# Attention: scores directly behind the transposes of the probabilities, wider products, small products at the end of the iteration

## The chip, the cores and the metric

The kernel runs on one core of one Trainium2 chip. The metric is the time of the device for one execution, in microseconds, as the median of several runs. Three runs of the kernel before took 557.59, 556.81 and 554.96 us.

## The reference

Sliding-window attention with sink tokens is followed by a soft mixture of experts and a feed-forward layer, all in fp32:

```python
scores = (q @ k.T) / 8                      # B=4, H=8, S=768, D=64
keep = (pos_k < 4) | ((0 <= pos_q - pos_k) & (pos_q - pos_k < 128))
a = softmax(where(keep, scores, -1e9));  x = a @ v           # x: 3072 x 512
logits = x @ phi                            # 3072 x 32 slots (8 experts of 4)
d = softmax(logits, over tokens);   slot_in = d.T @ x
slot_out[e] = relu(slot_in[e] @ w1[e]) @ w2[e]               # w1: 512 x 1024
x = softmax(logits, over slots) @ slot_out
h = x @ w_in;   out = (h - tanh(h)) @ w_out                  # d_ff = 2048
```

With a window of 128, a tile of 128 queries needs the keys of its own tile and of the tile before, and the 4 sink keys.

## The kernel before, in words

**Stages.** The attention stage works on pairs of heads, 16 in all (4 batches of 4 pairs). While it runs, expert weights are loaded into slots of a ring. Behind it come the experts' first product (`ffn1`, L1000), which frees slots for the remaining weights (`refill`, L968), the second (L1106), and the feed-forward layer (L1258 and around it).

**Iterations.** The attention loop (L760) has 48 iterations, three to a pair; each handles two query tiles of 128 for both heads. It is written as a pipeline in which the engines get their instructions in the order of the code, and each engine runs its own in that order. Iteration `i` issues, in this order:

- `trans(i-4)` (L661): four 128x128 transposes of normalized probabilities on TensorE into the one buffer `pT`; VectorE multiplies them by the two triangle masks (L667) and copies the middle blocks (L670). `pb_of` says where this goes.
- `exps(i-2)` (L621): on ScalarE, four exponentials with sums (L628) and two small operations.
- `turn_tasks` (L547): transposes of x (`x_trans`, L337) from a queue `xq`, each with a copy by ScalarE (L343), and those steps of a batch's tail that are transposes.
- a step of the conversion of `w_in` on VectorE and ScalarE (`conv_step`).
- `do_logits` (L724): the logits of a finished pair (L351), added up by VectorE (L356).
- `run_tasks` (L556): the other steps of a batch's tail: products with sink values, maximum, exponentials, slot inputs (L432, L437).
- `scores(i)` (L560): the products of queries and keys into two of the three buffers `sc`.
- `copies(i)` (L600): the scores go to SBUF with the window's masks (L611 on ScalarE, L612 and L608 on VectorE), and VectorE takes the maximum (L618).
- `norm(i-2)` (L633): a reciprocal on VectorE and the multiplication by it on GpSimd (L640).
- `avs(i-5)` (L672): the products of probabilities and v, which add up in two banks over the three iterations of a pair; behind the third, ScalarE copies them out (L709) and the pair is queued for logits one iteration later and for transposes of x two later.

The small products share two buffers of PSUM, `mi` (`misc`, L314): a third one waits until the first has been copied out.

**Shapes.** Scores are products of 64x64 quadrants (two heads by two row halves, four run side by side). For the first half of a tile's queries one matmul takes all of its two or three key blocks of 66 columns (64 keys and 2 sinks), with an output in steps; for the second half there is one matmul of 66 columns to a block. In `avs`, a block of v (`own`) is the weight for the probabilities of its own tile and of the next one, partly as one matmul of 128 columns and partly as two of 64; the blocks of v with their halves swapped (`other`, from `swapped`) take the middle blocks. In fp32 each matmul is two MATMUL and two LDWEIGHTS instructions.

Of the kernel before, what the change touches and what calls it, by code (L numbers as in the profile page):

```python
# [28 lines left out]
P = 128  # L29
SINK, WIN = 4, 128  # L30
CH = P + SINK
KW = 6 * CH + 2
HB = CH // 2
# [94 lines left out]
def tile_kernel(ctx: ExitStack, tc: tile.TileContext, qk, vv, v0, v0t, nw, phi, w1, w2,  # L128
# [17 lines left out]
    def run(ctx, fast):  # L146
# [35 lines left out]
        def sv(slot, lo, n, dt=F32):  # L182
            if slot in HALF:
                return slots[slot][lo // 1024][:, lo % 1024:lo % 1024 + n].bitcast(dt)
            return slots[slot][0][:, lo:lo + n].bitcast(dt)
# [59 lines left out]
        def attention(fast):  # L245
            nqk = {}
            swapped = [{}, {}]
            VS = (((11, 1552, 0, 3), (12, 1584, 3, 3)), ((10, 1536, 0, 4), (11, 768, 4, 2)))
            with ExitStack() as c2:
                ap = c2.enter_context(tc.tile_pool(name="ap", bufs=1))  # L250

# [279 lines left out]
                def kslc(a, lo, n):  # L531
                    return a[:, S + lo:S + lo + n]

                NQ = B * NP_ * 3

                def pb_of(i):
                    return sv(10, 768 * (i % 3), 768) if i % 3 < 2 else sv(11, 0, 768)

                Zs, sc_t, av, small, sus = {}, {}, {}, {}, {}

# [1 line left out]
                cur = [[]]  # L542
# [4 lines left out]
                def turn_tasks():  # L547
                    n = 0
                    while cur[0] and cur[0][0].__name__ in ("t_pst", "t_trd", "t_trl"):
                        cur[0].pop(0)()  # L550
                        n += 1
                    while n < 2 and xq and xq[0][0] <= now[0] and xq[0][1] <= done[0] and len(xq) > 2 * n:
                        xq.pop(0)[2]()
                        n += 1

                def run_tasks():  # L556
                    while cur[0]:
                        cur[0].pop(0)()

                def scores(i):  # L560
                    pb, m = divmod(i, 3)
                    a = nqk[pb][0]
                    n = (i + ZO) % 5
                    z = z4 if n == 4 else sv(11, 1024, 4 * CH) if n == 3 else sv(12, 4 * CH * n, 4 * CH)
                    Zs[i] = z
                    sc_t[i] = [pp.tile([P, 512], F32, name="sc", tag="sc", bufs=3) for u in range(2)]
                    for jj in range(2):
                        for n in range(3):
                            for u in range(2):
                                t = 2 * m + u  # L570
                                lo = CH * (t - 1) + (CH + 2 if t == 0 and jj else 68 if jj else 0)
                                if t == 0 and jj == 0:
                                    lo = 0
                                s_ = sc_t[i][u]
                                if jj == 0:
                                    if n:
                                        continue
                                    k, o = (3 if t else 2), 0
                                    dst = [[CH, k], [1, HB]]
                                    w_ = HB * k  # L580
                                else:
                                    if t == 0 and n == 2:
                                        continue
                                    o = (198, 66)[n] if t == 0 else (330, 198, 66)[n]
                                    dst = [[1, HB]]
                                    lo, w_ = lo + HB * n, HB
                                j = 2 * t + jj
                                for hh in range(2):
                                    r, w = (slice(64 * x, 64 * x + 64) for x in (hh, hh ^ u))
                                    d = s_[w, o:]  # L590
                                    PE.matmul(bass.AP(d.tensor, d.offset, [list(d.ap[0])] + dst), a[r, 64 * j:64 * j + 64],  # L591
                                              kslc(a, lo, w_)[r, :], start=True, stop=True)

                def halves(x, o, n):
                    return bass.AP(x.tensor, x.offset + o, [list(x.ap[0]), [2 * CH, 2], [1, n]])
# [65 lines left out]
                def trans(i, tag="pT"):  # L661
                    Z = Zs.pop(i)
                    pt = pp.tile([P, 512], F32, name=tag, tag=tag, bufs=1 if tag == "pT" else 3)
                    for n in range(4):
                        PE.transpose(pt[:, P * n:P * n + P], Z[:, CH * n + 2:CH * n + 130], ident)  # L665
                    d = pb_of(i)
                    DVE.tensor_tensor(d[:, 0:512].rearrange("p (l c) -> p l c", l=2),  # L667
                                      bass.AP(pt.tensor, pt.offset, [list(pt.ap[0]), [0, 2], [1, 256]]),
                                      c_t[:, C_ML:C_ML + 512].rearrange("p (l c) -> p l c", l=2), op=ALU.mult)
                    DVE.tensor_copy(d[:, 512:768], pt[:, 256:512])  # L670

                def avs(i):  # L672
                    pb, m = divmod(i, 3)
                    b, p = divmod(pb, NP_)
                    v, vs, d = nqk[pb][1], swapped[pb % 2], pb_of(i)
                    if m == 0:
                        av[pb] = [pp.tile([P, 512], F32, name=f"av{x}", tag=f"av{x}", bufs=1) for x in range(2)]
                    t0 = 2 * m

                    def mm(a, w, src, u, n=1):  # L680
                        for hh in range(2):
                            k, r = (slice(64 * x, 64 * x + 64) for x in (a, hh))
                            x = d[k, src + P * u + 64 * (hh ^ u):]
                            x = bass.AP(x.tensor, x.offset, [list(x.ap[0]), [256 + P + 64 - P * hh, n], [1, 64]])
                            o = 64 * (t0 + u)
                            PE.matmul(av[pb][a][r, o:o + 64 * n], w(k, r), x, start=m == 0 and n == 2, stop=m == 2 and src == 512,  # L686
                                      skip_group_check=True)

                    def own(t):
                        return lambda k, r: v[k, t, r]  # L690

                    def other(t):
                        return lambda k, r: vs[t][k, r]

                    for a in range(2):
                        mm(a, own(t0), 0, 0, 2)
                    for a in range(2):
                        mm(a, own(t0 + 1), 0, 1)
                    if m:
                        for a in range(2):  # L700
                            mm(a, own(t0 - 1), 256, 0)
                    for u in range(2):
                        for a in range(2):
                            if t0 + u - 1 + a >= 0:
                                mm(a, other(t0 + u - 1 + a), 512, u)
                    if m == 2:
                        x = xt_t[p]
                        for a in range(2):
                            ACT.copy(x.rearrange("p (t a c) -> p a t c", a=2, c=64)[:, a],  # L709
                                     av[pb][a][:, 0:384].rearrange("p (t c) -> p t c", c=64))  # L710
                        xT[b, p] = x
                        lq.append((i + LAG + 1 + LD, b, p))
                        xq.append((i + LAG + 1 + XD, b, lambda: x_trans(b, p, 0, 4)))
                        xq.append((i + LAG + 1 + XD, b, lambda: x_trans(b, p, 4, 2)))
                        if p == NP_ - 1:
                            if b < B - 1:
                                a, late2[:] = tail_tasks(b)
                                steps.extend(a)
                                if b < B - 2:
                                    steps.append([lambda: done.__setitem__(0, b + 1)])  # L720
# [3 lines left out]
                def do_logits():  # L724
                    if lq and lq[0][0] <= now[0]:
                        logits(*lq.pop(0)[1:])
# [33 lines left out]
                for i in range(NQ):  # L760
                    now[0] = i
                    next_step()
                    k = i - LAG
# [2 lines left out]
                    k -= 1  # L766
                    if i >= 2:
                        exps(i - 2)
                    turn_tasks()
                    while stage[0] < min(3 * NC + 1, (i - 2) * CVR):  # L770
                        conv_step(stage[0])
                        stage[0] += 1
                    do_logits()
                    run_tasks()
                    scores(i)
                    if i < NQ - 3:
                        filler(sc_t[i][1], NE_ if i < NK else NF)
# [20 lines left out]
                    if k >= 0:  # L798
                        avs(k)
                        if k % 3 == 2 and k // 3 + 2 < B * NP_:  # L800
                            load_v(k // 3 + 2)
                    if i % 3 == 1 and pre:
                        ring_dma(pre.pop(0))
                    if i % 3 == 0 and i // 3 < 16 - NC:
# [656 lines left out]
```

## Time and profile before

| | |
|---|---|
| median of three runs | 556.81 us |
| the profiled execution | 558.53 us |
| its span | 556.7 us |
| mean granted clock of TensorE, as a share of full speed | 0.981 |

One execution was profiled. Times count from the start of its span. PE is TensorE's matmuls and PEld its weight loads, which lie over each other; DVE is VectorE, ACT ScalarE, POOL GpSimd, and SP issues the transfers. `out<-in` are the program's names without buffer numbers (`w` is a slot of the ring, which attention uses for its buffers too; `mi`, `sc`, `av`, `pT` are PSUM). Square brackets give the idle time ahead of a group and what ended it; "issue" means that the engine waited for nothing that the profile shows.

### The profile page before, as it was taken

The page shows a single profiled execution, that of the slowest core. Times are in us where ns is not written, and L with a number is a line of the kernel's source. Part 1 is how long each engine was busy: PE and PEld are TensorE (multiplying, and loading weights), DVE is VectorE, ACT ScalarE, POOL GpSimd, SP SyncE. Part 2 cuts the span into 40 slices and gives each one's busy share as a digit, 9 for nine tenths or more (in the row PEclk, how much of TensorE's full clock was granted, in tenths as well). Part 3 has the DMA queues.
Part 4 walks back from the last instruction along what each step waited for, and adds up shares of the span by engine and source line. Part 5 has one row for each costly group of instructions (what it writes and reads, how often), then busy time and mean ns, then how long its engine had stood idle before and what let it go on. Part 6 is the DMA issues. An engine that isn't in the chain of part 4 may idle for free.

```text
span 556.7 us, 14342 instructions
## 1 busy us (share of the span) xinstructions
PE 502.6 (90%) x5634; PEld 378.2 (68%) x5634; DVE 367.2 (66%) x752; ACT 301.8 (54%) x924; POOL 270.6 (49%) x337
## 2 busy tenths in 40 slices
PE   8788778778788989888999999999999999999996
PEld 5566665666666643325677777788888888888884
DVE  3598785878868648769998887545454454445441
ACT  4689886878889535245654554434343343334331
POOL 0465845746564300005878887654443443443441
PEclk9799998989989999999999999999999999999999
DMA  8988987454447889994223000210020010001002
GB/s 304 414 308 312 334 326 262 157 161 167 149 161 288 294 328 377 408 410 145 83 75 114 2 1 1 88 64 1 0 77 1 1 70 7 1 1 76 1 1 79
DMA packets 26618, 84.16 MB, mean 151 GB/s; under 512 B 3378, under 2 KB 7602, under 8 KB 24626
## 3 DMA queue, kind: packets, MB, share of 16 engines
q1 hardware_dynamic: 26546, 83.20, 41.1%
q8 instruction: 45, 0.74, 0.5%
q14 instruction: 27, 0.22, 0.1%
HBM read 76.90 MB, written 6.29 MB: 149 GB/s over the span
## 4 chain that ended last, share of the span: by engine, by line
PE 65%; DMA 10%; DVE 9%; ACT 7%; POOL 4%; issue 4%; SPq 1%; POOLq 0%; ACTq 0%; DVEq 0%
PE o L1258 42%; DMA w<-in_w 7%; PE sc L591 5%; PE h L1168 4%; PE av L686 3%; PE pT L665 3%; ACT w L628 2%; POOL w L640 2%; DMA w<-in_vv 1%; ACT xt L709 1%; PE mi L432 1%; DVE mx L618 1%; DVE g L1237 1%; DMA w<-in_w_in 1%; DVE y L1235 1%
## 5 line engine op out<-in xcount | busy, mean ns | idle before, releaser
L1223 POOL TENSOR_TENSOR gl<-g,gh 128x512 fp32r<-128x512 f32 x96 | 124.0, 1292 | 119.8 <-ACT gh L1222 119.0
L1258 PE MATMUL o<-whi,gh 128*128 128x512 f32 x384 | 152.0, 396 | 4.1 <-POOL wlo L1069 1.2
L1258 PE MATMUL o<-wlo,gh 128*128 128x512 f32 x384 | 151.1, 394 | 1.7 <-POOL wlo L1069 1.7
L1218 ACT ACTIVATE u<-h 128x512 f32<-128x512 f32 x96 | 57.5, 599 | 147.5 <-PE h L1168 147.4
L1235 DVE SCALAR_TENSOR_TENSOR y<-u,h 128x512 f32<-128x512 f32 x96 | 66.7, 695 | 100.3 <-ACT u L1218 100.3
L1258 PE MATMUL o<-whi,gl 128*128 128x512 f32 x384 | 108.3, 390 | 0.1
L1258 PEld LDWEIGHTS o<-whi,gh 128*128 128x128 f32 x384 | 72.3, 188 | 23.5 <-POOL wlo L1069 1.5
L1258 PEld LDWEIGHTS o<-wlo,gh 128*128 128x128 f32 x384 | 72.2, 188 | 18.8 <-POOL wlo L1069 2.4
L1258 PEld LDWEIGHTS o<-whi,gl 128*128 128x128 f32 x384 | 72.1, 188 | 16.2 <-POOL gl L1223 0.8
L640 POOL TENSOR_TENSOR w<-w,su 128x528 f32<-128x528 f32 x38 | 41.2, 1084 | 67.3 <-DVE su L635 52.1
L1237 DVE SCALAR_TENSOR_TENSOR g<-u,y 128x512 f32<-128x512 f32 x96 | 65.8, 685 | 7.0
L1222 ACT CAST gh<-g 128x512 fp32r<-128x512 f32 x96 | 58.9, 613 | 5.7 <-DVE g L1237 5.5
L628 ACT ACTIVATE w<-w,nb 128x132 f32<-128x132 f32 x152 | 59.7, 394 | 1.2
L591 PE MATMUL sc<-w 64*64 64x66 f32 (+2 forms) x1472 | 49.5, 262 | 5.9 <-DVE w L608 2.8
L591 PEld LDWEIGHTS sc<-w 64*64 64x64 f32 x1472 | 39.7, 140 | 21.5 <-issue 12.4
L686 PE MATMUL av<-w,w 64*64 64x64 f32 (+1 forms) x1408 | 42.3, 243 | 7.0 <-issue 7.0
L686 PEld LDWEIGHTS av<-w,w 64*64 64x64 f32 x1408 | 36.4, 141 | 9.1 <-issue 8.4
L1068 POOL TENSOR_SCALAR whi<-wf 128x512 fp32r<-128x512 f32 x16 | 9.9, 620 | 63.0 <-DMA w<-in_w_out 59.3
L1168 PE MATMUL h<-cT,wst 96*128 96x512 f32 x96 | 37.8, 395 | 0.9 <-DVE wst L1156 0.9
L611 ACT COPY w<-sc 128x264 f32<-128x264 f32 x63 | 21.5, 378 | 27.5 <-PE sc L591 19.2
L665 PE MATMUL pT<-c_t,w 128*128 128x128 f32 x148 | 25.9, 298 | 9.1 <-POOL w L640 7.1
L667 DVE TENSOR_TENSOR w<-pT,c_t 128x512 f32<-128x512 f32 x46 | 30.6, 666 | 4.0 <-PE pT L665 3.9
(250 smaller groups left out, 731.3 us busy)
## 6 DMA issues: line engine op xcount, KB each, us to landing
w<-in_w SPq DMA_DIRECT2D x32, 512.0 KB, 10.2
w<-in_w SPq DMA_DIRECT2D x14, 1024.0 KB, 8.1
w<-in_qk SPq DMA_DIRECT2D x16, 781.0 KB, 6.0
w<-in_w_out SPq DMA_DIRECT2D x15, 512.0 KB, 3.6
w<-in_vv SPq DMA_DIRECT2D x16, 384.0 KB, 4.7
w<-in_w_in SPq DMA_DIRECT2D x8, 512.0 KB, 4.6
w<-in_vv SPq DMA_DIRECT2D x16, 192.0 KB, 5.8
out<-xt SPq DMA_DIRECT2D x12, 256.0 KB, 2.1
```

Of the source, the lines that this page charges most:

```text
L591: PE.matmul(bass.AP(d.tensor, d.offset, [list(d.ap[0])] + dst), a[r, 64 * j:64 * j + 64], kslc(a, lo, w_)[r, :], start=True, stop=True)
L628: ACT.activation(z, z, AF.Exp, bias=nb[:, u:u + 1], scale=SCALE, accum_out=su[:, u, :])
L640: (POOL if i < NQ - 1 else DVE).tensor_tensor(z, z, f, op=ALU.mult)
L665: PE.transpose(pt[:, P * n:P * n + P], Z[:, CH * n + 2:CH * n + 130], ident)
L686: PE.matmul(av[pb][a][r, o:o + 64 * n], w(k, r), x, start=m == 0 and n == 2, stop=m == 2 and src == 512, skip_group_check=True)
L1168: PE.matmul(h_of(s), w_of(f), cT[0:G3, CK * c:CK * c + CK], start=True, stop=True)
L1218: ACT.activation(u_b[s % 3], h_of(s), AF.Square)
L1222: ACT.copy(gh, g)
L1223: POOL.tensor_tensor(gl, g, gh.bitcast(F32), op=ALU.subtract)
L1235: DVE.scalar_tensor_tensor(y_t, u, c0 / c1, h, op0=ALU.add, op1=ALU.mult)
L1237: DVE.scalar_tensor_tensor(g, u, c1, y_t, op0=ALU.mult, op1=ALU.mult)
L1258: PE.matmul(acc[t], a[:, P * t:P * t + P], w, start=start, stop=stop)
```

## The change

In the loop, the order within an iteration is now: transposes of the probabilities, exponentials, conversion, scores, copies, normalization, products with v, then logits, the other steps of the tail, and last the transposes of x and of the tail. `run_tasks` leaves the transposing steps to `turn_tasks`, which comes behind it. The second half of a tile's scores is one matmul with an output of steps downward, instead of two or three. In the products with v every block but the last is one matmul of 128 columns over its own and the next tile; for that the masked probabilities of a pair lie in one buffer `lu` and the product of a third tile moves to the next iteration. The middle blocks have buffers of their own (`mid_of`). The swapped v of odd pairs is in one place and comes with one transfer instead of two.

```diff
-            VS = (((11, 1552, 0, 3), (12, 1584, 3, 3)), ((10, 1536, 0, 4), (11, 768, 4, 2)))
+            VS = (((11, 1552, 0, 3), (12, 1584, 3, 3)), ((11, 256, 0, 6),))
...
-                def pb_of(i):
-                    return sv(10, 768 * (i % 3), 768) if i % 3 < 2 else sv(11, 0, 768)
+                lu = sv(10, 0, 1536)
+
+                def mid_of(m):
+                    return sv(10, 1536 + 256 * m, 256) if m < 2 else sv(11, 0, 256)
...
                 def run_tasks():
-                    while cur[0]:
+                    while cur[0] and cur[0][0].__name__ not in ("t_pst", "t_trd", "t_trl"):
                         cur[0].pop(0)()
...
+                        for u in range(2):
+                            t = 2 * m + u
+                            n = 3 if t else 2
+                            lo = CH * max(t - 1, 0) + (0, 68 if t else 2)[jj]
+                            for hh in range(2):
+                                r, w = (slice(64 * x, 64 * x + 64) for x in (hh, hh ^ u))
+                                d = sc_t[i][u][w, (0, CH * n - HB)[jj]:]
+                                PE.matmul(bass.AP(d.tensor, d.offset, [list(d.ap[0]), [(CH, -CH)[jj], n], [1, HB]]),
+                                          a[r, 64 * (2 * t + jj):64 * (2 * t + jj) + 64], kslc(a, lo, HB * n)[r, :],
+                                          start=True, stop=True)
...
                     def own(t):
-                        return lambda k, r: v[k, t, r]
...
+                        f = 512 * (t // 2) + P * (t % 2)
+                        n = 2 if t < 5 else 1
+                        g = 512 * ((t + 1) // 2) + 256 + P * ((t + 1) % 2)
+                        for a in range(2):
+                            for hh in range(2):
+                                k, r = (slice(64 * x, 64 * x + 64) for x in (a, hh))
+                                o, q = (64 * (hh ^ (x % 2)) for x in (t, t + 1))
+                                x = lu[k, f + o:]
+                                PE.matmul(av[pb][a][r, 64 * t:64 * t + 64 * n], v[k, t, r],
+                                          bass.AP(x.tensor, x.offset, [list(x.ap[0]), [g + q - f - o, n], [1, 64]]),
+                                          start=t == 0, stop=False, skip_group_check=True)
...
                     if m:
...
+                        own(2 * m - 1)
+                    own(2 * m)
+                    if m == 2:
+                        own(5)
                     for u in range(2):
...
+                        mid(2 * m + u)
...
                     if i >= 2:
                         exps(i - 2)
-                    turn_tasks()
                     while stage[0] < min(3 * NC + 1, (i - 2) * CVR):
                         conv_step(stage[0])
                         stage[0] += 1
-                    do_logits()
-                    run_tasks()
                     scores(i)
...
                         avs(k)
                         if k % 3 == 2 and k // 3 + 2 < B * NP_:
                             load_v(k // 3 + 2)
+                    do_logits()
+                    run_tasks()
+                    turn_tasks()
```

## Rows read from the trace of the kernel before

**Rows 1.** The page, busy us, share and instructions; then ScalarE's busy tenths in 40 slices

```profile
PE 502.6 (90%) x5634; PEld 378.2 (68%) x5634; DVE 367.2 (66%) x752; ACT 301.8 (54%) x924; POOL 270.6 (49%) x337
...
ACT  4689886878889535245654554434343343334331
```

**Rows 2.** The chain that ended last, 181 to 262 us: start us, us, what

```profile
204.30 1.92 PE o L1000 x16
207.58 8.55 DMA w<-in_w
...
236.94 10.17 DMA w<-in_w
247.16 1.90 PE cvt L1106 x10
```

**Rows 3.** Busy times of two stretches: us, each engine's busy us (instructions), clock, transfers

```profile
63.60:178.87 115.27, 92.50 (x2388) 72.82 (x2384) 90.25 (x241) 94.68 (x406) 66.30 (x118) 0.96 0.63 217
20.00:63.60 43.60, 36.55 (x930) 29.90 (x928) 36.75 (x94) 35.98 (x155) 27.34 (x51) 0.89 0.92 331
```

**Rows 4.** Groups of TensorE's instructions, 63.60 to 178.87 us: busy us, mean ns | idle before

```profile
L591 PE MATMUL sc<-w 64*64 64x66 f32 (+2 forms) x920 | 30.1, 260 | 1.6 <-issue 1.0 <-DVE w L608 0.5
```

**Rows 5.** ScalarE's waits, 63.60 to 178.87 us: for whom, us in total, times, longest

```profile
ACT w L611 <- PE sc L591: 12.6, 8, 2.7
ACT xt L709 <- PE av L686: 3.8, 2, 2.1
ACT z L611 <- PE sc L591: 0.8, 3, 0.4
```

**Rows 6.** Timeline of one iteration, TensorE and ScalarE: start us, us, group, [idle before]

```profile
100.39 0.82 PE L342 MATMUL mi<-c_t,xt 128*128 128x128 f32 x6
...
102.34 0.84 ACT L343 COPY x<-mi 128x512 f32<-128x512 f32 x2
...
102.96 0.63 PE L351 MATMUL mi<-xt,phi_t 128*32 128x256 f32 x6 [1.75 <-ACT x L343]
...
103.53 0.92 PE L591 MATMUL sc<-w 64*64 64x198 f32 x32
...
104.53 0.66 ACT L611 COPY w<-sc 128x264 f32<-128x264 f32 x2 [1.34 <-PE sc L591]
```

**Rows 7.** ScalarE's waits, 20 to 63.6 us

```profile
ACT w L611 <- PE sc L591: 5.2, 5, 1.8
...
ACT xt L709 <- PE av L686: 0.6, 1, 0.6
```

**Rows 8.** TensorE's groups by shape in one iteration, 154.62 to 156.24 us

```profile
L591 PE MATMUL sc<-w 64*64 64x198 f32 x8 | 0.6, 353 | 0.0
L591 PE MATMUL sc<-w 64*64 64x66 f32 x24 | 0.5, 218 | 0.0
L686 PE MATMUL av<-w,w 64*64 64x64 f32 x20 | 0.5, 218 | 0.0
...
L686 PE MATMUL av<-w,w 64*64 64x128 f32 x8 | 0.4, 270 | 0.0
```

**Rows 9.** Timeline of TensorE: the products with v of one iteration, the 66-column scores of another

```profile
138.76 0.75 PE L686 MATMUL av<-w,w 64*64 64x128 f32 x28
...
149.81 0.53 PE L591 MATMUL sc<-w 64*64 64x66 f32 x24
```

**Rows 10.** Timeline of TensorE: an interrupted block of products with v

```profile
72.53 0.39 PE L686 MATMUL av<-w,w 64*64 64x128 f32 x5
74.48 0.90 PE L686 MATMUL av<-w,w 64*64 64x128 f32 x35 [1.56 <-issue]
```

**Rows 11.** Busy times between one restart of TensorE and the next, columns as in rows 3

```profile
62.54:68.26 5.72, 4.46 (x127) 3.51 (x127) 4.31 (x12) 5.16 (x22) 3.95 (x8) 1.00 0.94 319
...
81.01:87.31 6.30, 4.37 (x128) 3.41 (x127) 5.74 (x16) 3.97 (x17) 4.57 (x8) 1.00 0.80 326
```

**Rows 12.** Waits of TensorE's weight loads, 63.60 to 178.87 us

```profile
PEld pT L665 <- POOL w L640: 5.1, 7, 1.4
```

More of the change, by code (lines that the diff above doesn't have):

```diff
@@ L567, in scores @@
                     for jj in range(2):
[L568 to L592, printed above, removed]
+                        for u in range(2):
[8 more added lines that the diff above has]
+                                          start=True, stop=True)
                 def halves(x, o, n):
@@ L665, in trans @@
                         PE.transpose(pt[:, P * n:P * n + P], Z[:, CH * n + 2:CH * n + 130], ident)
-                    d = pb_of(i)
-                    DVE.tensor_tensor(d[:, 0:512].rearrange("p (l c) -> p l c", l=2),
+                    m = i % 3
+                    DVE.tensor_tensor(lu[:, 512 * m:512 * m + 512].rearrange("p (l c) -> p l c", l=2),
                                       bass.AP(pt.tensor, pt.offset, [list(pt.ap[0]), [0, 2], [1, 256]]),
                                       c_t[:, C_ML:C_ML + 512].rearrange("p (l c) -> p l c", l=2), op=ALU.mult)
-                    DVE.tensor_copy(d[:, 512:768], pt[:, 256:512])
+                    DVE.tensor_copy(mid_of(m), pt[:, 256:512])
                 def avs(i):
@@ L674, in avs @@
                     b, p = divmod(pb, NP_)
-                    v, vs, d = nqk[pb][1], swapped[pb % 2], pb_of(i)
+                    v, vs = nqk[pb][1], swapped[pb % 2]
                     if m == 0:
                         av[pb] = [pp.tile([P, 512], F32, name=f"av{x}", tag=f"av{x}", bufs=1) for x in range(2)]
[L678 to L687, printed above, removed]
@@ L689, in own @@
-                    def own(t):
-                        return lambda k, r: v[k, t, r]
[L692 to L698, printed above, removed]
+                    def own(t):
+                        f = 512 * (t // 2) + P * (t % 2)
[9 more added lines that the diff above has]
+                                          start=t == 0, stop=False, skip_group_check=True)
@@ new lines, in mid @@
+                    def mid(t):
+                        for a in range(2):
+                            if t - 1 + a < 0:
+                                continue
+                            for hh in range(2):
+                                k, r = (slice(64 * x, 64 * x + 64) for x in (a, hh))
+                                o = P * (t % 2) + 64 * (hh ^ (t % 2))
+                                PE.matmul(av[pb][a][r, 64 * t:64 * t + 64], vs[t - 1 + a][k, r], mid_of(m)[k, o:o + 64],
+                                          start=False, stop=t == 5, skip_group_check=True)
@@ L699, in avs @@
                     if m:
-                        for a in range(2):
-                            mm(a, own(t0 - 1), 256, 0)
+                        own(2 * m - 1)
+                    own(2 * m)
+                    if m == 2:
+                        own(5)
                     for u in range(2):
-                        for a in range(2):
-                            if t0 + u - 1 + a >= 0:
-                                mm(a, other(t0 + u - 1 + a), 512, u)
+                        mid(2 * m + u)
```

## The prediction

> **What bounds the kernel now.** I read the page first, then the chain of waits, the busy times by stretch, and who waited for whom inside the stretch that the change touches. The page says that TensorE is busy nine tenths of the span and ScalarE half [rows 1]. That average is misleading. ScalarE's digits are 8 and 9 in the first third and 3 to 5 after it: the attention stage and the feed-forward stage have different limits, and only the first is edited.
>
> The chain shows what a gain in attention would be worth. After the last products with v come the first expert product at 204.30 us, four stretches of weight loading from 207.58 to 247.11 us (first and last shown), and then the feed-forward stage [rows 2]. The loads start when the first expert product has freed slots, and everything behind them hangs on them in a fixed order. So the later stages move as a block: what the attention loop loses or gains is what the span loses or gains.
>
> Inside the loop, 63.60 to 178.87 us [rows 3] holds 920 MATMULs of scores [rows 4]; a pair of heads has 92 in three iterations, so these are 10 pairs, 30 iterations of 3.84 us. ScalarE is busy 94.68 of 115.27 us and TensorE 92.50, of which part is matmuls lying over each other. ScalarE comes nearest to being full, and its idle time is concentrated: 13.4 us stand ahead of the copies of the scores (L611), until the scores are there, and 3.8 us ahead of the copies of the products with v (L709) [rows 5]. These 17.2 us are most of the 20.6 us in which it does nothing.
>
> Where the 13.4 us come from is seen in one iteration [rows 6]. Behind the transposes of the probabilities, TensorE transposes x (L342, 100.39 us) into both buffers of the small products. The logits (L351) need one of these back, and ScalarE copies it out at 102.34 us, behind its exponentials. TensorE stands still 1.75 us, does the logits at 102.96 and only then the scores at 103.53. Now it is ScalarE's turn to stand still: 1.34 us, until 104.53. Two engines wait for each other in turn, since small products that nobody needs soon stand ahead of the scores that ScalarE needs next.
>
> **The change part by part.**
>
> *Order.* Scores go directly behind the transposes; logits, tail steps and transposes of x go behind the products with v. In the iteration of [rows 6] the scores could start where L342 does, some three microseconds earlier. ScalarE is in its exponentials then, so the copies would find them ready. This answers each of the 8 + 3 waits behind the 13.4 us. Bounds: nothing, if the scores are late for another reason; 13.4 us, if all go. I take three quarters, 10.0 us: some of these waits also have an interrupted instruction stream in them (below), which stays. What is late next is ScalarE's own work, 94.68 us in this stretch.
>
> In 20 to 63.6 us the same wait sums to 5.2 us in 5 places [rows 7]. Part of it is the start of the pipeline, and the transfers are busy 0.92 of that stretch [rows 3], so I take half: 2.5 us, between 0 and 5.2.
>
> *Fewer matmuls.* Per pair of heads the scores go from 46 to 24 matmuls and the products with v from 54 to 46; in fp32 each is two MATMUL and two LDWEIGHTS instructions. Over 16 pairs 960 MATMULs of 3200 go. But the columns stay the same: three of 66 become one of 198, two of 64 become one of 128. Durations by shape [rows 8]: 66 columns 218 ns and 198 columns 353 (mean), 64 columns 218 and 128 columns 270; so 64 more columns cost 52 ns, which is what a 66-column matmul costs beyond its fixed part. And the fixed part overlaps: 24 of 66 columns lie in 0.53 us [rows 9]; without the last one's 0.218 that is 0.31 us for five steps of four quadrants, 62 ns a step. Three such steps are 187 ns against about 165 for one of 198 columns (66 columns are 54 ns by the row above). There are two replacements in an iteration, so the scores gain 0.04 us. The products with v gain in one iteration of three what they lose in another, since a whole tile's product moves to the third. That is under 2 us of TensorE time over 48 iterations. It lies beside ScalarE's exponentials, and I cost it at nothing; with ScalarE out of the way it would be 2 us.
>
> The Trainium skill (TensorE: Matmul & The Clock Gate, Part 1) says that from start to start matmuls never come closer than about 25 ns, however small. By that the 960 would be an estimated 24 us of TensorE time instead of 2. With so much off TensorE the first rival below, in which every wait goes, would be the likeliest. The row disagrees, at about 15 ns each within a step of four.
>
> *Instruction stream.* Some blocks stop in the middle with nothing to wait for: five products with v, then 1.56 us of "issue", then the other 35 [rows 10]. The four stretches from one such restart to the next (first and last shown) hold 127 or 128 matmuls and 127 weight loads each [rows 11]. So the stop comes every 256 instructions or so: TensorE runs out of loaded code, and a dense burst reaches the end of a block before the next has arrived. The stretch of [rows 3] has 4772 of these instructions in 10 pairs, 477 a pair; 120 fewer is a quarter fewer such ends. ScalarE's waits on L709 come from these stops: 3.8 us late [rows 5] and 0.6 early [rows 7]. A quarter is 1.2 us. Bounds: 0 to 4.4, as each stop depends on where a block ends.
>
> The Trainium skill (Runtime: NRT & Kernel Launch, Instruction fetch mechanics) agrees on blocks of 256 instructions, but calls crossing one mostly hidden. By that this term would be zero and the sum 1.2 us smaller; the 1.56 us stop says that it is not hidden here.
>
> *A new wait.* ScalarE's copies of the transposed x (L343) and of the tail steps stood behind its exponentials, which gave TensorE over 2 us to produce their source. Now they stand behind the copies of the scores, 0.66 us [rows 6], and TensorE has the products with v (0.75 us [rows 9]) and up to 0.82 us of transposes [rows 6] to do. Queued behind such a copy are the next iteration's exponentials, and behind these all of the softmax. If TensorE ends the scores just as ScalarE arrives, the wait is 0.75 + 0.82 - 0.66 = 0.9 us; if ScalarE is that much late itself, it is nothing. Transposes of x occur in the loop for 12 pairs, and some three tail copies behave alike: 0 to 14 us. With the scores earlier ScalarE is more often the late one, so I take 2.5 us, nearer the lower end.
>
> *The rest.* The masked probabilities and middle blocks go to other places with the same two VectorE operations. SP's order stays, with one load of v less for every second pair. Neither is on the path.
>
> **The sum.** -10.0 - 2.5 - 1.2 + 2.5 = -11.2 us. The profiled execution took 558.53 us (span 556.7), so 547.3 by it; the median of the three runs is 1.7 us lower, so 545.6.
>
> **The rivals.**
>
> *Everything goes (18%).* TensorE runs so far ahead that the stops are covered too. Then all of 13.4 + 3.8 late and 5.2 + 0.6 early goes, and the new wait never shows: 23 us, 534. For it: the late stretch has transfers at 0.63 and both engines under 0.83. Against it: VectorE has 90.25 us of work in the same stretch [rows 3], behind the same copies.
>
> *Transfers hold the first half back (14%).* Early in the loop attention shares the transfer engines with weight loads; they are 0.92 busy in 20 to 63.6 us [rows 3], so a loop that is a tenth faster has nothing left there, and q and k come late. The early term goes and half of the late one: -5.0 - 1.2 + 1.0, 551.6.
>
> *The wait moves to the normalization (13%).* The transposes wait for GpSimd's multiplication (L640), 5.1 us in the late stretch [rows 12]. That multiplication follows the copies of the scores through maximum, exponentials and reciprocal. If this ring of work sets the pace, the scores, now directly behind the transposes, inherit the wait and only 2 us are left: 555.
>
> *Slower (13%).* The wait on L343 at its upper price. It decides when ScalarE reaches the end of its copies less than 0.9 us behind the end of the scores: then each of some 15 places costs its full 0.9, 14 us. With the gain halved to 5.0 + 1.2 + 1.2 = 7.4 that is +6.6, 563. For it: in [rows 6] ScalarE is at the scores the moment that they end. Against it: it is there because it was starved, which the new order ends.
>
> **How the numbers follow.** The forecast has 42%, with its own range of 541 to 550. A measurement of this kernel tells about 0.5% (2.8 us) from no change. Faster by more holds for the forecast, for everything goes and for the transfers: 74%. Within: the normalization, 13%. Slower: 13%. The range from 535 to 558 leaves out most of the slower case and the far half of the first rival, under 2 in 10.
>
> **What would show it.** In the profile after: waits of L611 for the scores under 5 us in all, logits no longer waiting for ScalarE, the last scores some 11 us earlier, the four weight loads as long as before and earlier by as much, the block of scores still above 0.8 us, and stops still every 256 instructions but a quarter rarer. A wait of L343 for the transposes of x is the new cost: above 6 us in sum, my estimate of it was wrong. The prediction is wrong if the loop doesn't shorten while L611 stops waiting (the normalization), or if the loop shortens and the weight loads don't move.

## The result: 542.24 us against 557.2, and the profile after

The changed kernel took 542.24 us (median of 4 runs, 541.41 to 543.64), the kernel before on the same occasions 557.2 (4 runs, 554.96 to 559.13): a ratio of 0.9735 with an interval of 0.9692 to 0.9779. I had forecast 545.6, in a range of 535 to 558. The profiled execution took 542.7 us with a span of 540.9, 15.8 us less than before. Every ratio leaves out executions more than 1.5% above the fastest of their kernel.

First the page of the kernel after: busy us, share and instructions, ScalarE's digits, and the queue that brings code to the engines (packets, MB, share).

```profile
PE 495.5 (92%) x4674; PEld 370.2 (68%) x4674; DVE 366.7 (68%) x752; ACT 300.9 (56%) x924; POOL 272.6 (50%) x337
...
ACT  4689999998986333546544554443443343334431
...
q8 instruction: 38, 0.62, 0.5%
```

Against [rows 1], 960 MATMULs are gone, and the other engines have the same work. ScalarE's digits show the effect: 9 where there were 6 to 8, and the drop to 3 comes a slice earlier. The code queue moved 45 packets before and 38 now.

The busy times of the same 30 iterations in the kernel after, columns as in [rows 3]:

```profile
60.99:163.95 102.96, 88.31 (x1784) 68.47 (x1784) 89.71 (x237) 95.02 (x409) 68.24 (x120) 1.00 0.69 243
20.00:60.99 40.99, 34.83 (x702) 27.67 (x701) 36.61 (x96) 35.95 (x157) 27.51 (x49) 0.97 0.95 358
```

The late stretch is 12.3 us shorter, the early one 2.6. ScalarE does the same work, 95.02 us, but now fills 92% of the late stretch instead of 82%.

ScalarE's and the weight loads' waits in the late stretch of the kernel after (us in total, times, longest):

```profile
PEld pT L652 <- POOL w L627: 10.6, 10, 2.1
...
ACT x L343 <- PE mi L342: 3.4, 5, 1.3
...
ACT w L598 <- PE sc L577: 1.6, 2, 0.8
...
ACT z L598 <- PE sc L577: 0.9, 1, 0.9
```

L598 is L611 of before, L652 is L665, L627 is L640 and L577 is L591. The 12.6 + 0.8 us for the scores [rows 5] are 2.5 now; the 3.8 us for the products with v are gone. L343 is new, and the transposes wait for GpSimd twice as long as in [rows 12].

One iteration of the kernel after on TensorE (start us, us, group, idle before), to be held against [rows 6]:

```profile
97.27 0.60 PE L652 MATMUL pT<-c_t,w 128*128 128x128 f32 x4
97.80 0.90 PE L577 MATMUL sc<-w 64*64 64x198 f32 x16
98.52 0.73 PE L675 MATMUL av<-w,w 64*64 64x128 f32 x24
99.07 0.41 PE L686 MATMUL av<-w 64*64 64x64 f32 x16
99.41 0.44 PE L342 MATMUL mi<-c_t,xt 128*128 128x128 f32 x2
100.86 0.33 PE L652 MATMUL pT<-c_t,w 128*128 128x128 f32 x1 [1.01 <-POOL w L627]
```

ScalarE copies these scores here, in the same kernel:

```profile
100.61 0.64 ACT L598 COPY w<-sc 128x264 f32<-128x264 f32 x2
```

The scores were there at 98.70, and the copy came 1.9 us later with no wait. In [rows 6] ScalarE stood waiting 1.34 us for them. It is TensorE that stands now, for GpSimd, and ScalarE doesn't.

The groups of the scores and of the logits in the late stretch (count | busy us, mean ns | idle before); neither waits any more:

```profile
L577 PE MATMUL sc<-w 64*64 64x198 f32 (+1 forms) x480 | 29.5, 332 | 0.1
...
L351 PE MATMUL mi<-xt,phi_t 128*32 128x256 f32 x60 | 6.3, 391 | 0.0
```

And the chain of the kernel after behind the loop, to [rows 2]:

```profile
187.27 1.92 PE o L990 x16
...
189.79 12.04 PE o L990 x109
201.83 11.12 DMA w<-in_w
213.01 8.02 DMA w<-in_w
...
236.80 0.49 PE h L1158
```

The first expert product starts 17.0 us earlier than in [rows 2]; 15.8 us of that are left in the span. The stages behind moved nearly as a block.

### The profile page after: what moved, and what is told of

Same layout as the page of the kernel before. It is cut to its first block, busy times and chain, and to the rows that moved or that the text cites. A ratio compares the mean times of both kernels' runs of the same rounds, so it can differ in the third digit from the quotient of the medians.

```text
span 540.9 us, 12411 instructions
## 1 busy us (share of the span) xinstructions
PE 495.5 (92%) x4674; PEld 370.2 (68%) x4674; DVE 366.7 (68%) x752; ACT 300.9 (56%) x924; POOL 272.6 (50%) x337
## 4 chain that ended last, share of the span: by engine, by line
PE 63%; DVE 12%; ACT 10%; DMA 6%; POOL 5%; issue 2%; SPq 0%; POOLq 0%; ACTq 0%; DVEq 0%
PE o L1248 43%; PE h L1158 4%; DMA w<-in_w 4%; ACT w L615 3%; PE o L990 3%; PE sc L577 2%; PE pT L652 2%; DVE mx L605 2%; DMA w<-in_w_in 1%; DMA w<-in_qk 1%; PE av L675 1%; DVE g L1227 1%; PE cvt L1096 1%; ACT x L343 1%; ACT w L598 1%
## 5 line engine op out<-in xcount | busy, mean ns | idle before, releaser
L627 POOL TENSOR_TENSOR w<-w,su 128x528 f32<-128x528 f32 x38 | 41.7, 1098 | 49.3 <-DVE su L622 38.1
L577 PE MATMUL sc<-w 64*64 64x198 f32 (+1 forms) x768 | 49.0, 335 | 4.3 <-DVE w L595 3.1
L577 PEld LDWEIGHTS sc<-w 64*64 64x64 f32 x768 | 27.9, 133 | 15.7 <-issue 5.8
L652 PE MATMUL pT<-c_t,w 128*128 128x128 f32 x148 | 24.0, 286 | 15.4 <-POOL w L627 11.9
L675 PE MATMUL av<-w,w 64*64 64x128 f32 (+1 forms) x768 | 34.2, 263 | 0.1
L652 PEld LDWEIGHTS pT<-c_t,w 128*128 128x128 f32 x148 | 16.3, 144 | 22.0 <-POOL w L627 16.8
L675 PEld LDWEIGHTS av<-w,w 64*64 64x64 f32 x768 | 29.9, 133 | 1.7 <-issue 0.6
```

Of the source, the lines that this page charges most:

```text
L577: PE.matmul(bass.AP(d.tensor, d.offset, [list(d.ap[0]), [(CH, -CH)[jj], n], [1, HB]]), a[r, 64 * (2 * t + jj):64 * (2 * t + jj) + 64], ksl ...
L627: (POOL if i < NQ - 1 else DVE).tensor_tensor(z, z, f, op=ALU.mult)
L675: PE.matmul(av[pb][a][r, 64 * t:64 * t + 64 * n], v[k, t, r], bass.AP(x.tensor, x.offset, [list(x.ap[0]), [g + q - f - o, n], [1, 64]]), s ...
```

## The experiments

**One account for all of them.** For each profiled execution the table gives, from 20 us to the loop's end, ScalarE's waits for TensorE (the rows "ACT ... <- PE ..." of the waits, summed), TensorE's stops for "issue" in the same stretch, and the start of the first expert product. "Code" is the packets of the code queue. The ratio is to the kernel before, timed beside it, with its interval; waits, stops and the first expert product are of the one profiled execution, which for e11_sc (547.41 us) was the longest of six.

| kernel | median us | ratio | code | PE stops, us | ACT waits for PE, us | first expert product |
|---|---|---|---|---|---|---|
| before | 557.2 | | 45 | 10.9 | 25.0 | 204.30 |
| after | 542.24 | 0.9735 (0.9692 to 0.9779) | 38 | 1.2 | 11.2 | 187.27 |
| e1_order | 551.41 | 0.9909 (0.9878 to 0.9939) | 45 | 10.4 | 19.0 | 197.81 |
| e2_merge | 548.95 | 0.9874 (0.9849 to 0.9899) | 38 | 0 | 16.7 | 193.67 |
| e11_sc | 544.42 | 0.9772 (0.9736 to 0.9808) | 40 | 2.6 | 14.1 | 191.82 |
| e4_split | 558.37 | 1.003 (1.0005 to 1.0055) | 49 | 17.8 | 25.2 | 202.78 |
| e5_pad | 573.09 | 1.0247 (1.0184 to 1.031) | 50 | 10.9 | 30.8 | 217.01 |
| e6_padctl | 549.05 | 0.9871 (0.9834 to 0.9908) | 41 | 3.6 | 13.4 | 192.16 |
| e9_wide | 551.1 | 0.9893 (0.9861 to 0.9925) | 41 | 0 | 15.3 | 195.41 |
| e7_shift | 555.14 | 0.9965 (0.993 to 1.0) | 46 | 7.2 | 19.6 | 197.36 |
| e3_xfront | 541.62 | 0.974 (0.9711 to 0.9769) | 38 | 1.3 | 6.5 | 184.35 |
| e8_norm | 541.31 | 0.9723 (0.9691 to 0.9755) | 38 | 0 | 10.3 | 187.08 |
| e10_both | 538.84 | 0.9671 (0.9639 to 0.9702) | 38 | 0.7 | 6.9 | 184.67 |

From the kernel before to the one after the waits fall by 13.8 us and the first expert product comes 17.0 us earlier; the other kernels lie along the same line, within some 3 us but for e5_pad, where TensorE stops for another 5.2 us at 203.05 us, behind the stretch of the table. So the time of the loop reads as ScalarE's work plus its waits for TensorE. That is an account of where the time lies; what makes the waits is the question of the runs below.

**The change in halves.** e1_order is the kernel before with the new order alone (`run_tasks` leaves the transposing steps to `turn_tasks` as in the change):

```diff
-                    turn_tasks()
...
-                    do_logits()
-                    run_tasks()
                     scores(i)
...
+                    do_logits()
+                    run_tasks()
+                    turn_tasks()
```

> The order of the new kernel with the matmuls and buffers of the kernel before: only the small products and the transposes of x move behind the products with v. Theory A (the gain is the order: ScalarE no longer starves for the scores): ScalarE's waits for the scores in the loop fall from 18.6 us to under 5, and at least 11 of the 15 us come: ratio 0.975 to 0.981. Rival B (the gain is the smaller instruction stream): the stops in the middle of dense blocks stay, and with all dense work in one burst they even get longer; under 6 us come: ratio above 0.989.

It gave 0.9909, 5.1 us: the time that rival B expected. e2_merge is the kernel after with these lines put back in the old order, so it has the fewer instructions alone, with the new buffers and the single load of v that go with them:

> The wide products of the new kernel in the old order. Theory A: the columns stay the same, so little comes: 0 to 3 us from a quarter fewer stops, ratio 0.994 to 1.0, and ScalarE's waits for the scores stay above 12 us. Rival B: at least 8 of the 15 us come, ratio under 0.986.

It gave 0.9874, 7.0 us: more than theory A allowed and less than rival B asked. The halves sum to 12.1 us and the whole gave 14.8; the intervals are too wide to call that more than a sum. The half that I had priced at 1.2 us is at least as large as the half that I had priced at 12.5. ScalarE's waits in the loop of e1_order show what happened to the latter:

```profile
ACT x L343 <- PE mi L342: 7.6, 7, 3.5
...
ACT w L611 <- PE sc L591: 5.4, 4, 1.7
ACT xt L709 <- PE av L686: 3.5, 3, 1.5
```

The waits for scores fall from 19.8 us to 7.6 (5.4 here and 2.2 in smaller rows), not to under 5 as expected. But 7.6 us of waits on L343 take their place. In e2_merge the waits for scores stay, since the order is the old one, and still 7 us are gone:

```profile
ACT w L598 <- PE sc L577: 13.3, 10, 2.5
```

**Is it the instructions, or the time of the matmuls?** In e4_split the kernel after gets its scores back in matmuls of 66 columns, all of them, 68 a pair instead of 24:

```diff
-                        for u in range(2):
+                        for c in range(3):
+                            for u in range(2):
...
-                                PE.matmul(bass.AP(d.tensor, d.offset, [list(d.ap[0]), [(CH, -CH)[jj], n], [1, HB]]),
-                                          ..., kslc(a, lo, HB * n)[r, :], ...)
+                                    PE.matmul(sc_t[i][u][w, o:o + HB], ..., kslc(a, lo, HB)[r, :], ...)
```

> The new kernel with all scores in matmuls of 66 columns: per pair 68 matmuls of scores instead of 24 (before: 46), the same columns, the same order. That is 2816 more instructions of TensorE in the attention stage, 11 more blocks of 256. Theory A: TensorE gets some 3 us more of work behind ScalarE's exponentials and stays ahead: at most 3 us slower than the new kernel, ratio 0.973 to 0.979. Rival B: stops of 1 to 2 us for each block come back in dense work and ScalarE feels most of them: 8 us or more slower, ratio above 0.987.

The whole gain is gone: 1.003. The new order, the new buffers and the single load of v are all still there, so none of them makes the gain by itself. A block of scores of e4_split on TensorE has three times the matmuls of the block shown above, and lasts as long, 0.93 us to 0.90:

```profile
100.29 0.93 PE L580 MATMUL sc<-w 64*64 64x66 f32 x48
```

In undisturbed iterations, the whole stretch from the first product of the scores to the last with v differs by less than 0.1 us between the two kernels. So the 16 us between the two kernels aren't the matmuls' own time. The stops rise with it, from 1.2 to 17.8 us, and ScalarE's waits from 11.2 to 25.2. The waits in the loop of e4_split:

```profile
ACT x L343 <- PE mi L342: 13.3, 9, 3.6
...
PE av L689 <- issue: 7.5, 4, 3.2
ACT w L601 <- PE sc L580: 6.7, 6, 2.2
PE sc L580 <- issue: 6.3, 6, 1.9
```

e11_sc is e1_order with the wide scores of the kernel after, while the products with v stay as before:

```diff
-                                    PE.matmul(bass.AP(d.tensor, d.offset, [list(d.ap[0])] + dst), ..., kslc(a, lo, w_)[r, :], ...)
+                                PE.matmul(bass.AP(d.tensor, d.offset, [list(d.ap[0]), [(CH, -CH)[jj], n], [1, HB]]),
+                                          ..., kslc(a, lo, HB * n)[r, :], ...)
```

> The kernel of the new order alone, with the scores in wide matmuls too but the products with v and their buffers as before: 1408 of the 1920 instructions of TensorE that the change saves. If the time follows the number of instructions between the order alone (0.991) and the whole change (0.9735), it is at 1408/1920 of the way: ratio 0.975 to 0.982. If it is the products with v that matter (their stops were the long ones), it stays near 0.988 or above.

0.9772: of the 9.7 us from e1_order to the kernel after, the scores' fewer instructions bring 7.6.

Then instructions were added to the kernel after that compute nothing of use. e5_pad puts 32 matmuls of one column ahead of each iteration's products with v (64 MATMULs and weight loads, 0.46 us from the first start to the last):

```diff
+                    for n in range(32):
+                        w, hh = n % 4 // 2, n % 2
+                        k, r = (slice(64 * x, 64 * x + 64) for x in (w, hh))
+                        PE.matmul(av[pb][w][r, 400:401], z_t[k, 0:64], z_t[k, 0:1],
+                                  start=m == 0 and n < 4, stop=False, skip_group_check=True)
```

> The new kernel with 32 needless bf16 matmuls of one column ahead of the products with v in each iteration, into columns that nobody reads: 64 more instructions of TensorE an iteration, about as many as in the kernel with split scores, and almost no columns. If the supply of code is what the wide products relieved, TensorE stops in the middle of dense blocks again (over 8 us of issue in the loop against 1.2) and the time goes up by 8 us or more over the new kernel: ratio above 0.988. If it is the columns and fixed costs of the matmuls themselves, at most 3 us come: ratio under 0.980.

e6_padctl was to be its control, the same place filled by few instructions (4 matmuls of 128 columns in fp32, 16 instructions):

```diff
+                        PE.matmul(av[pb][w][r, 384:512], ident[k, 0:64], ident[k, 0:128],
```

> Control to the padded kernel: 4 needless fp32 matmuls of 128 columns in the same place, 16 instructions an iteration in place of 64, with about as much work for the array or more. If the supply of code decides, under 3 us over the new kernel: ratio 0.972 to 0.979. If TensorE's time decides, at least as slow as the padded kernel.

e5_pad gave 1.0247 and e6_padctl 0.9871, slower than expected. That doesn't settle it, since the control adds less time: in undisturbed iterations, the stretch from the first product of the scores to the last with v is 0.33 to 0.48 us longer than in the kernel after in e5_pad, and only 0.21 to 0.26 us in e6_padctl. e9_wide has 288 columns with zero weights, which add 0.45 to 0.49 us in the same 16 instructions:

```diff
+                        PE.matmul(av[pb][w][r, 224:512], z_t[k, 0:128].bitcast(F32), c_t[k, C_ID:C_ID + 288],
```

> A better control to the padded kernel, whose 32 small matmuls took 0.46 us of TensorE between the scores and the products with v. Here 4 needless fp32 matmuls of 288 columns (weights of zero) stand in the same place: about 0.48 us, but 16 instructions an iteration instead of 64, which is 8 blocks of code fewer over the loop. If TensorE's time alone made the padded kernel slow (573 us), this one is as slow: ratio 1.015 to 1.035. If the supply of code had a part in it, it is at least 6 us faster than the padded one, ratio under 1.013, and interrupted blocks are nearly gone (under 3 us against some 14).

0.9893 against e5_pad's 1.0247: with no more time on TensorE, 48 instructions more in each of 48 iterations (nine blocks of code) cost some 20 us. How they cost it is not wholly separated: e5_pad stops for 10.9 us in the loop and 5.2 us behind it, and its mean granted clock is 0.976 against 0.994. But e9_wide itself is 8.8 us slower than the kernel after, for 23 us of matmuls: TensorE's time is not free there either, though it has no stops.

**What a stop depends on.** Up to the restart that [rows 10] shows at 74.48, and up to the corresponding restart of e1_order and of e4_split, this many instructions had run (busy times, columns as in [rows 3]):

```profile
0.00:74.40 74.40, 59.52 (x1363) 46.20 (x1363) 53.35 (x135) 55.83 (x234) 36.63 (x68) 0.93 0.92 336
```

```profile
0.00:74.65 74.65, 59.96 (x1363) 46.14 (x1363) 51.54 (x133) 55.01 (x233) 36.24 (x67) 0.93 0.91 334
```

```profile
0.00:68.60 68.60, 51.50 (x1364) 41.59 (x1365) 44.45 (x116) 47.11 (x198) 29.05 (x58) 0.95 0.89 324
```

And this is what TensorE restarts with, in e1_order and in e4_split:

```profile
74.73 0.78 PE L686 MATMUL av<-w,w 64*64 64x128 f32 x33 [0.74 <-issue]
```

```profile
68.70 0.64 PE L580 MATMUL sc<-w 64*64 64x66 f32 x29 [0.72 <-issue]
```

1363 matmuls and as many weight loads, 2726 (2729 in e4_split), in three programs, two of which are in the products with v there and one in the scores, at 68.7 to 74.7 us. The place of a stop is a number of instructions, not an operation. Counted with the few other instructions of TensorE's queue (mostly for semaphores), all 57 such stops above 0.15 us from 20 to 210 us of the 13 traces stand 193 beyond a multiple of 256.

The packets of the code queue, taken one by one, show what ends a stop. Each packet holds 16384 bytes, and each of the 57 stops ends 2.2 to 2.7 us after such a packet began to move: the one of [rows 10] at 74.48, after a packet that began at 71.95 and had arrived at 73.03. They show as well which blocks end in a stop. Between 20 and 180 us the 13 traces have 307 ends of blocks. Where the transfers were at least 0.7 busy during the block, 45 of the 83 blocks that TensorE went through in under 6 us (the stop left out) end in a stop, and 4 of the 92 slower ones; where the transfers were less busy, 4 of 132. So a stop comes where TensorE is through a block before the next one is there, and most often beside dense transfers. No run took the transfers away, so their part is read, not tested.

e7_shift moves the stops by half a block, with 64 one-column matmuls (128 instructions) in one early iteration of the kernel before:

```diff
+                    if i == 3:
+                        m_ = misc()
+                        for n in range(64):
+                            k = slice(64 * (n % 2), 64 * (n % 2) + 64)
+                            PE.matmul(m_[k, 0:1], z_t[k, 0:64], z_t[k, 0:1], start=True, stop=True)
```

> The kernel before with 64 needless matmuls of one column (128 instructions, half a block of 256) behind the scores of the fourth iteration, where TensorE waits anyway. If the stops are ends of blocks of code, each stop moves 128 instructions earlier in the program, so that other matmuls are interrupted than before; the restarts stay 254 to 256 instructions apart. The time may go either way by up to 4 us, as other places are hit. If the stops belong to what is executed there (a buffer, a bank, a transfer), they stay at the same matmuls.

One of its stops is at the same number of instructions, 2727, of which 128 are the added ones:

```profile
0.00:69.80 69.80, 56.12 (x1363) 44.57 (x1364) 50.03 (x130) 53.95 (x227) 35.77 (x66) 0.93 0.94 345
```

```profile
69.92 0.57 PE L686 MATMUL av<-w,w 64*64 64x64 f32 x21 [1.92 <-issue]
```

So it interrupts other matmuls than before, as expected of ends of blocks. The time is 0.9965, with an interval that touches 1: this shift of the stops is worth 2 us (0 to 4) of the 15. (Its profiled execution, 551.85 us, was one of its shorter ones.)

**The new waits.** e3_xfront puts `turn_tasks()` of the kernel after back to its old place, which takes away the wait on L343; e8_norm lets the normalization go ahead of the copies, for the transposes' wait for GpSimd; e10_both is both. The edit of e3_xfront:

```diff
+                    turn_tasks()
                     while stage[0] < min(3 * NC + 1, (i - 2) * CVR):
...
                     run_tasks()
-                    turn_tasks()
```

and of e8_norm:

```diff
+                    if i >= 2:
+                        norm(i - 2)
                     copies(i)
...
-                    if i >= 2:
-                        norm(i - 2)
```

> The new kernel, but the transposes of x and the transposing tail steps go back ahead of the scores; logits and the other tail steps stay behind the products with v. If the 4.3 us that ScalarE waits with its copies of the transposed x in the new kernel are a real cost, they vanish and the scores come only 0.2 to 0.4 us later, which ScalarE's lateness hides: 2 to 4 us faster than the new kernel, ratio 0.966 to 0.970. If ScalarE's waits there are only another form of the pace that GpSimd's normalization sets (14.3 us of waits of the transposes in the new kernel), the time stays: ratio 0.971 to 0.977.

> The new kernel with the normalization (reciprocal on VectorE, multiplication on GpSimd) ahead of the copies of the scores in each iteration, so that VectorE does the reciprocal before and not behind the maximum. What is late in the new kernel are the transposes, which wait 15.9 us for that multiplication. If this ring sets the pace of the loop, these waits fall under 8 us and 3 to 6 us come: ratio 0.962 to 0.968. If ScalarE's own work sets it, the waits fall and the time stays: ratio 0.971 to 0.976.

> The new kernel with both changes that took away its largest remaining waits one at a time and left the time alone: transposes of x ahead of the scores again, and the normalization ahead of the copies. If the two waits covered for each other, 3 us or more come: ratio under 0.968. If ScalarE's own work or TensorE's time sets the pace, the time stays: ratio 0.970 to 0.976.

e3_xfront: the waits on L343 are gone, the profiled execution was 3 us shorter (539.77), the median is 541.62, and the ratio, 0.974, is that of the kernel after. e8_norm: the transposes' wait fell from 15.9 us in the loop to 3.0, and the time is the same, 0.9723. The weight loads of the transposes stand for something else then:

```profile
PEld pT L652 <- issue: 13.3, 18, 1.8
...
PEld pT L652 <- POOL w L627: 3.0, 4, 1.7
```

So neither wait alone sets the pace. e10_both has the best median of all, 538.84 us, and a ratio of 0.9671 (0.9639 to 0.9702). It beats the kernel before; that it beats the kernel after is likely, but the intervals overlap, and the two were not timed together.

## Why the prediction was right, and which term was not

The time was within the forecast's own range, and the waits that were forecast to go went. The sum was 3.4 us short, and that it came so near is partly luck. The order with its new wait was forecast at 12.5 - 2.5 = 10.0 us and brought 5.1 alone and 7.7 on top of the fewer instructions (from e2_merge to the kernel after). The instructions were forecast at 1.2 us and brought 7.0 alone and 9.7 on top of the order. The two errors have opposite signs.

*Order, -12.5 us.* Right for the waits, too large for the time. The waits for the scores fell by 14.4 us in the loop (19.8 to 5.4) with the whole change and by 12.2 with the order alone, but only 5.1 to 7.7 us of time came, as other waits took their place (7.6 us on L343 in e1_order). In the kernel after the 5.4 us are just above the 5 that I had named as the sign. The early stretch gained 2.6 us beside transfers that were 0.95 busy, so the rival in which transfers hold it back didn't come.

*Fewer matmuls' own time, 0.* Right: the block of scores is 0.90 us against 0.92 in [rows 6], and three times as many matmuls take 0.93. The rule of 25 ns from start to start (the Trainium skill, TensorE: Matmul & The Clock Gate, Part 1) would put the 48 MATMULs of e4_split in an estimated 1.2 us; they lie in 0.93, so between quadrants side by side it doesn't hold.

*The instruction stream, -1.2 us: the step that failed.* It read: "120 fewer is a quarter fewer such ends. ScalarE's waits on L709 come from these stops ... A quarter is 1.2 us. Bounds: 0 to 4.4". A quarter of the 4.4 us is 1.1, not 1.2, which changes nothing. But both halves of the working were too small. The stops didn't shrink by a quarter: 10.9 us of them became 1.2, nine tenths. And they cost more than the waits on L709, since what TensorE issues behind a stop comes late too, the next scores among it. e2_merge shows how much: with the order as before, the waits on the products with v fell by 4.6 us (5.2 to 0.6) and those for the scores by 3.9 (19.8 to 15.9). Measured alone the term is 7.0 us, outside my bounds. What the trace of the kernel before shows behind each stop, and who waits for that, was the place to read the second half.

*The new wait, +2.5 us.* 4.3 us in 7 places in the kernel after, under the 6 that I had set as the limit, and taking it away alone brought nothing that the medians show. But it grows with whatever makes TensorE late behind the scores: it is 7.6 us with the old number of instructions (e1_order), 13.3 with more (e4_split), and 7.6 with longer matmuls and no stop at all (e9_wide). The slower rival's place was right, but the trigger that it named, ScalarE at the end of its copies close behind the scores, was not the only one: 8.4 of the 13.3 us in e4_split are three waits in which TensorE stops. With the stream of e4_split the change would have been no gain.

*The normalization.* The wait came, 15.9 us in the loop, but not as a price: ScalarE was busy meanwhile, and e8_norm took it away for nothing. Only with the new wait gone as well (e10_both) did the median fall, by 3.4 us.

*The stages behind.* They moved by 15.8 of 17.0 us. The weight loading looks different: two loads in the chain instead of four, behind twelve unbroken microseconds of expert products.

The one stop in the loop of the kernel after stands at the end of a block too. The prediction's step from a quarter fewer ends of blocks to a quarter fewer stops failed because most ends don't stop: in the kernel before 10 of some 26 did. The rule that crossing a block is mostly hidden (the Trainium skill, Runtime: NRT & Kernel Launch, Instruction fetch mechanics) fits the kernel after, with 1.2 us, and not the one before, with 10.9.

TensorE's granted clock doesn't explain the gain of the fewer instructions: e2_merge has a mean of 0.981 like the kernel before and is 7.0 us faster. Nor is it enough: e9_wide has 0.994 like the kernel after and is 8.8 us slower. But from e2_merge to the kernel after it rose from 0.981 to 0.994 with the order, and its part in those 7.7 us isn't separated.

Why did nine tenths of the stops go with a quarter of the instructions? The number of blocks alone isn't it (e9_wide, 41, has none; e6_padctl, 41, has 3.6 us of them). The time that TensorE takes for a block goes with it: from 20 to 180 us a block took 6.0 us in the mean before and 7.1 after, and the kernels with means of 6.6 us or more have 0 to 3.6 us of stops, those with 5.4 to 6.0 have 7.2 to 17.8. That fits the counts above, where blocks of under 6 us stop and longer ones hardly do. What delays a code packet beside dense transfers stays open.

## What to carry to other kernels

When two engines wait for each other in turn, put what the fuller one needs next first; here that was worth a third to a half of the gain. Count the instructions of a dense engine as a cost of their own: rows of "issue" in the middle of a block, at equal numbers of instructions, say that wider matmuls over the same columns can pay even where they save no time on the engine. Such stops can go much faster than the instructions do, once a block takes the engine longer than the next one takes to come. A stop is priced by everything issued behind it, not by the one wait next to it.

## What was not expected of the hardware

- From 38 to 49 packets of code, with the new order, the time rose by 1.5 us for each in the mean, and by 1.0, 1.5 and 1.7 from step to step (0.9735 at 38, 0.9772 at 40, 0.9909 at 45, 1.003 at 49); from e9_wide to e5_pad by 2.2.
- A matmul whose output has three steps downward through the bank costs about what its columns cost: 16 of the scores' MATMULs of up to 198 columns, half of them downward, lie in 0.90 us, 332 ns each in the mean against 353 for those of [rows 8], whose steps go upward.
- A stop of TensorE at the end of a block of 256 instructions lasts until 2.2 to 2.7 us after the next code packet began to move (57 stops in 13 traces).
- 48 fp32 MATMULs of 66 columns on quadrants lie in 0.93 us, 15 ns apart, with as many weight loads beside them.
